# A decode step on one core: last values in three parts, output blocks as rows of 512, one product for the bias

## The chip, the core and the metric

The kernel runs on one core of a Trainium2 chip. The core has a matrix engine (TensorE, "PE" in the profile, with its weight loads listed apart as "PEld"), a vector engine (VectorE, DVE), a scalar engine (ScalarE, ACT), GpSimd (POOL) and a queue engine (SyncE, SP) that here issues nearly all transfers from device memory. Sixteen DMA engines move the data. On-chip data lies in SBUF; TensorE writes its products to PSUM, from where VectorE or ScalarE fetch them. The metric is the device time of one execution in microseconds; a time for a kernel is the median of its runs.

## What is computed

One token of 512 values passes two branches. The attention branch, cut to what matters:

```python
q = (xn @ wq)                       # 32 heads of 128
k = k_cache[:, :, Sk - 4096:, :]    # the last 4096 rows of every head
v = v_cache[:, :, Sk - 4096:, :]
p = softmax(q . k * Dh ** -0.5)
o = p @ v                           # 32 heads of 128, side by side: 4096 values
s = o @ wo                          # 4096 x 512
out = x + s * silu(B(xn))
```

`xn` is the normalised token and `B` a small two-layer branch with weights of 512x512, 512x1376 and 1376x512. Every head has its own keys and values, all bf16: 32 heads x 4096 rows x 128 values for K and again for V are 64 MiB, and `wq` and `wo` add 4 MiB each.

## The kernel before

**Loads.** All large loads go through `load` (line 77) on SP's queue in program order: the weights of `B`, `wq`, and then, for each step `s`, the K tile of head pair `s` and the V tile of head pair `h = s - 3` (`LAG`). A K or V tile holds two heads as 128 partitions x 64 columns x 128 values, 2 MiB. There are six K buffers and three V buffers. The output weights `wo` come between them: the block of heads 0 to 15 (`load_wo(0)`, 2 MiB) and of heads 16 to 23 (`load_wo(1)`, 1 MiB) in K buffers that have become free, heads 24 and 25 spread over 64 partitions (`load_few`), and the rows of heads 26 to 31 two heads at a time (`load_rows`, 256 KiB each). The last V tile comes in two parts, 48 and 16 columns (`CUT`), with the rows of heads 28 and 29 between the two and those of heads 30 and 31 behind.

**Scores.** Of every K tile, `nd(s)` columns are multiplied with q and summed on VectorE (`k_vector`, lines 309 and 311) and the others are transposed on TensorE into a buffer `pt` of the pool `ps_tr`, which has three, copied out by ScalarE (`k_turn`, lines 324 and 325) and multiplied by q on TensorE (`k_scores`, line 330).

**Softmax.** For a group of four heads, `sm_max` makes the maximum of each partition; `sm_turn` turns it on TensorE (line 355), takes the maximum of each head (line 357) and lays the scaled maxima out as a small matrix `md` (line 360). `sm_exp` spreads it over the partitions with two products into one PSUM tile `mb_ps`: ones times `md` (line 368), and a fixed parity pattern `par_t` times a fixed matrix `neg` of 0 and -1e30 (line 370), so that each partition sees only the heads whose values it holds. ScalarE copies the tile out (line 373) and takes the exponentials p with it as bias (line 377). `sm_den` and `sm_rden` make the reciprocal of the sum.

**Values.** `v_pair` multiplies p by a V tile: for most pairs 64 products with a V column block as weights and 2 columns of p (line 441), for four pairs p as weights and 512 columns of V (line 430). `v_out` scales the result by the reciprocal, one ScalarE instruction a head (line 461), into the columns of `o_blk`.

**Output product.** Heads 0 to 15 and 16 to 23 are first rearranged (`ox_spread`, `ox_pick`), heads 24 and 25 (the few block) also through `ox_few`. Then there are two forms of multiplying by `wo`. `y_wide` (line 498), used for heads 0 to 15 alone, makes one product of 512 columns for each of its 16 weight rows, into a PSUM row that ScalarE copies to `y_row` (line 504). `rows_add` (line 149), used for everything else, makes four products of 128 columns into partitions 0, 32, 64 and 96 of a PSUM tile `y_ps`, which stays open until the last head. `y_block` calls it for a block, `y_head` for one head, and a last call adds `y_row` to `y_ps`.

**Order.** The loop over `s` stands in a region in which the order on TensorE, VectorE and ScalarE is the order of the text. The last three steps, which hold V tiles 13, 14 and 15, are the ones the change touches most:

```python
sm_turn(LG); ox_spread(few_block); y_block(1); sm_exp(LG); ox_pick(few_block)
rows_add(y_ps, one_f, y_row, False); v_pair(h, v); v_out(2 * h, 2); ox_few(few_block)
sm_den(LG); sm_rden(LG)
...
y_block(few_block); v_pair(h, v); v_out(2 * h, 2)
...
for r in range(h_part, h_part + 2): y_head(r)
v_pair(h, v, 0, CUT)
for r in range(h_part + 2, H - 2): y_head(r)
v_pair(h, v, CUT, CP); v_out(2 * h, 2)
for r in range(H - 2, H): y_head(r)
```

After the region, VectorE multiplies `y_ps` by the gate and adds x (lines 607 and 609), and SP stores the result.

Of the kernel before, what the change touches and what calls it, by code (L numbers as in the profile page):

```python
# [8 lines left out]
P = 128  # L9
# [14 lines left out]
EARLY = 4  # L24
LATE = 14
MOVED = (1, 3)
CUT = 48


@with_exitstack  # L30
def kernel(
# [39 lines left out]
    ps_o = ctx.enter_context(tc.tile_pool(name="ps_o", bufs=1, space=PSUM))  # L71
    ps_y = ctx.enter_context(tc.tile_pool(name="ps_y", bufs=1, space=PSUM))
    sm_pool = ctx.enter_context(tc.tile_pool(name="sm", bufs=3))
    wts_guard = tc.tile_pool(name="wts", bufs=1)
    wts = wts_guard.__enter__()

# [19 lines left out]
    def load_kv(pool, cache, i, cuts=None):  # L96
        t = pool.tile([P, CP, Dh], BF16, tag="kv", name="kv")
        src = cache[0, 2 * i:2 * i + 2, W0:, :].rearrange("a (b c) d -> b a (c d)", b=P // 2)
        dst = t[:].rearrange("p c d -> p (c d)")
        cuts = cuts or (0, CP)  # L100
        for c0, c1 in zip(cuts, cuts[1:]):
            load(dst[:, c0 * Dh:c1 * Dh], src[:, :, c0 * Dh:c1 * Dh])
            if c0 == 0 and c1 < CP:
                load_rows(H - 4, 2)
        return t

# [154 lines left out]
    for c in range(2):  # L261
# [10 lines left out]

    par = const.tile([P, 2], FP32, name="par")
    nc.vector.tensor_reduce(out=par[:], in_=ident_f[:].rearrange("p (b a) -> p a b", a=2), axis=AX.X,
                            op=ALU.max)
    par_t = const.tile([2, P // 2, 2], FP32, name="par_t")
    nc.vector.tensor_copy(out=par_t[:], in_=ident_f[0:2, 0:2].unsqueeze(1).to_broadcast([2, P // 2, 2]))
    neg = const.tile([2, 2, 2], FP32, name="neg")  # L280
    nc.vector.tensor_scalar(out=neg[:], in0=ident_f[0:2, 0:2].unsqueeze(1).to_broadcast([2, 2, 2]),
                            scalar1=-1.0, scalar2=1e30, op0=ALU.add, op1=ALU.mult)


# [66 lines left out]
    def sm_turn(g):  # L351

        s = st[g]
        mt_ps = ps_misc.tile([2, P], FP32, tag="misc", name="mt_ps")
        nc.tensor.transpose(mt_ps[:], s["m1"][:], ident_f[:])  # L355
        mx = sm_pool.tile([2, 2], FP32, tag="mx", name="mx")
        nc.vector.tensor_reduce(out=mx[:], in_=mt_ps[:].rearrange("r (b a) -> r a b", a=2), axis=AX.X,
                                op=ALU.max)
        s["md"] = sm_pool.tile([2, 2, 2], FP32, tag="md", name="md")
        nc.vector.scalar_tensor_tensor(out=s["md"][:],  # L360
                                       in0=ident_f[0:2, 0:2].unsqueeze(2).to_broadcast([2, 2, 2]),
                                       scalar=-scale, in1=mx[:].unsqueeze(1).to_broadcast([2, 2, 2]),
                                       op0=ALU.mult, op1=ALU.mult)

    def sm_exp(g):
        s = st[g]
        mb_ps = ps_misc.tile([P, G], FP32, tag="misc", name="mb_ps")
        nc.tensor.matmul(mb_ps[:], lhsT=ones_f[0:2, :], rhs=s["md"][:].rearrange("k r a -> k (r a)"),  # L368
                         start=True, stop=False)
        nc.tensor.matmul(mb_ps[:], lhsT=par_t[:].rearrange("k b a -> k (b a)"),  # L370
                         rhs=neg[:].rearrange("k r a -> k (r a)"), start=False, stop=True)
        mb = sm_pool.tile([P, G], FP32, tag="mb", name="mb")
        nc.scalar.copy(out=mb[:], in_=mb_ps[:])  # L373
        s["pT"] = sm_pool.tile([P, 2, CP, 2], BF16, tag="pT", name="pT")
        s["sum"] = sm_pool.tile([P, G], FP32, tag="sum", name="sum")
        for i in range(G):
            nc.scalar.activation(out=s["pT"][:, i // 2, :, i % 2], in_=s["S"][:, i // 2, :], func=ACT.Exp,  # L377
                                 scale=scale, bias=mb[:, i:i + 1], accum_out=s["sum"][:, i:i + 1])
# [73 lines left out]
    def v_out(h, n):  # L452
        g, hl = divmod(h, G)
        b = [i for i, (h0, _) in enumerate(blocks) if h >= h0][-1]
        if b not in o_blk:
            o_blk[b] = sm_pool.tile([P, blocks[b][1]], BF16, tag=f"o{b}", bufs=1, name="o")
            if b == few_block:
                nc.gpsimd.memset(o_blk[b][:], 0.0)
        c = h - blocks[b][0]
        for k in range(n):  # L460
            nc.scalar.mul(o_blk[b][:, c + k:c + k + 1], st[g]["oT"][:, hl + k:hl + k + 1],  # L461
                          st[g]["rden"][:, hl + k:hl + k + 1])
# [31 lines left out]


    y_row = small.tile([1, D], FP32, name="y_row")

    def y_wide(i):
        n = blocks[i][1]
        yr_ps = ps_misc.tile([1, D], FP32, tag="misc", name="yr_ps")  # L500
        for t in range(n):
            nc.tensor.matmul(yr_ps[:], lhsT=ox_blk[i][:, t:t + 1], rhs=wo_blk[i][:, t, :], start=(t == 0),
                             stop=(t == n - 1))
        nc.scalar.copy(out=y_row[:], in_=yr_ps[:])

    def y_block(i):
        for t in range(8):
            rows_add(y_ps, ox_blk[i][:, t:t + 1], wo_blk[i][:, t, :], False)

    def y_head(h):  # L510
        rows_add(y_ps, o_blk[few_block][:, h - few_h:h - few_h + 1], wo_row(h), h == H - 1)

    NP = H // 2
    LG = H // G - 1
    region = tc.manual_schedule(engines={mybir.EngineType.PE, mybir.EngineType.DVE,
# [3 lines left out]
    for s in range(NP + LAG):  # L519
        h = s - LAG  # L520
        last = h == NP - 1
        kn = load_kv(k_pool, A_k_cache, s) if s < NP else None
        if s == LAG:
            wts_guard.__exit__(None, None, None)
            v_pool = ctx.enter_context(tc.tile_pool(name="v", bufs=V_BUFS))
            wo_blk[few_block] = v_pool.tile([64, 8, D], BF16, tag="wo_few", bufs=1, name="wo_few")
            nc.gpsimd.memset(wo_blk[few_block][:], 0.0)
            wo_rows = v_pool.tile([P, H - h_part, D], BF16, tag="wo_rows", bufs=1, name="wo_rows")
        if last:
            load_rows(h_part, 2)  # L530
            v = load_kv(v_pool, A_v_cache, h, (0, CUT, CP))
        elif h >= 0:
            v = load_kv(v_pool, A_v_cache, h)
        if h in (7, 12):
            load_wo(h // 12)
        if h == 11:
            load_few()
        if last:
            load_rows(H - 2, 2)

        if s < NP:
            turn = [s // 2 - 1] if s % 2 == 0 and s > 0 else []
            k_open(s)
            k_vector(s, kn, 0)
            k_turn(s, kn)
            for g in turn:
                sm_turn(g)
            if s % 2 == 1 and s >= 3:
                sm_den((s - 3) // 2)
                sm_rden((s - 3) // 2)  # L550
            k_scores(s)
            if s % 2 == 1:
                sm_own(s // 2)
            for g in turn:
                sm_exp(g)
            if s in (12, 15):
                ox_spread(s // 14)
            if s == 11:
                v_add(3)
                v_out(12, 4)  # L560
            k_vector(s, kn, 1)
            if h >= 0:
                v_pair(h, v)
            if s in (12, 15):
                ox_pick(s // 14)
            if s == 13:
                y_wide(0)
            if s % 2 == 1:
                sm_max(s // 2)
            g = (h - 1) // 2  # L570
            if h > 0 and h % 2 == 1 and g not in MOVED:
                v_out(G * g, G)
            if h % 2 == 0 and h > 0 and g in MOVED and g != 3:
                v_add(g)
                v_out(G * g, G)
            if s == NP - 1:
                v_out(2 * h, 2)
        elif s == NP:

            sm_turn(LG)  # L580
            ox_spread(few_block)
            y_block(1)
            sm_exp(LG)
            ox_pick(few_block)
            rows_add(y_ps, one_f, y_row, False)
            v_pair(h, v)
            v_out(2 * h, 2)
            ox_few(few_block)
            sm_den(LG)
            sm_rden(LG)  # L590
        elif not last:
            y_block(few_block)
            v_pair(h, v)
            v_out(2 * h, 2)
        else:
            for r in range(h_part, h_part + 2):
                y_head(r)
            v_pair(h, v, 0, CUT)
            for r in range(h_part + 2, H - 2):
                y_head(r)  # L600
            v_pair(h, v, CUT, CP)
            v_out(2 * h, 2)
            for r in range(H - 2, H):
                y_head(r)
# [36 lines left out]
```

## Time and profile before

| | us |
|---|---|
| median of 4 runs | 195.93 (195.86 to 196.92) |
| the profiled execution | 196.05 |
| its span, first to last instruction | 194.3 |
| PE busy, of the span | 141.0 (73%) |
| DVE busy | 138.5 (71%) |
| ACT busy | 83.9 (43%) |
| moved by DMA | 79.16 MB, mean 407 GB/s |
| mean granted TensorE clock | 0.707 of full speed |

The profile is of one execution. Its page gives busy times over the whole span, slices of the span, the chain of work that ended last, and groups of instructions by source line with count, busy time, mean duration and the idle time before them. Further views of the same trace list instructions in order of time, the chain in order of time, and the busy time, granted clock and DMA share of any stretch. A matmul's listed duration includes its own latency, so that matmuls overlap in the list and the distance between starts is what one costs in a series. Times in what follows are microseconds from the start of the span.

### The profile page before, as it was taken

The page shows a single profiled execution, that of the slowest core. Times are in us where ns is not written, and L with a number is a line of the kernel's source. Part 1 is how long each engine was busy: PE and PEld are TensorE (multiplying, and loading weights), DVE is VectorE, ACT ScalarE, POOL GpSimd, SP SyncE. Part 2 cuts the span into 40 slices and gives each one's busy share as a digit, 9 for nine tenths or more (in the row PEclk, how much of TensorE's full clock was granted, in tenths as well). Part 3 has the DMA queues.
Part 4 walks back from the last instruction along what each step waited for, and adds up shares of the span by engine and source line. Part 5 has one row for each costly group of instructions (what it writes and reads, how often), then busy time and mean ns, then how long its engine had stood idle before and what let it go on. Part 6 is the DMA issues. An engine that isn't in the chain of part 4 may idle for free.

```text
span 194.3 us, 4894 instructions
## 1 busy us (share of the span) xinstructions
PE 141.0 (73%) x2188; PEld 112.0 (58%) x2188; DVE 138.5 (71%) x160; ACT 83.9 (43%) x183; POOL 6.2 (3%) x13
## 2 busy tenths in 40 slices
PE   0549779877787993497886979286767997959651
PEld 0444469867787943257885254086757556947540
DVE  1550119969489999999999998098999977881001
ACT  2003019887946905235746053161546057823000
POOL 2110007000000000000000000000000000000000
PEclk9999966797558699588555596855556697575555
DMA  5999899999999999999999999999999999999960
GB/s 212 403 498 432 381 425 425 427 425 432 425 432 425 427 425 432 432 425 432 425 432 428 432 432 422 428 432 428 425 428 422 432 425 432 422 435 423 413 265 2
DMA packets 6909, 79.16 MB, mean 407 GB/s; under 512 B 872, under 2 KB 1736, under 8 KB 2120
## 3 DMA queue, kind: packets, MB, share of 16 engines
q1 hardware_dynamic: 6736, 78.84, 95.6%
q8 instruction: 17, 0.28, 0.5%
q14 instruction: 4, 0.03, 0.0%
q10 hardware_dynamic: 152, 0.00, 0.0%
HBM read 78.84 MB, written 0.00 MB: 406 GB/s over the span
## 4 chain that ended last, share of the span: by engine, by line
DMA 42%; DVE 24%; PE 15%; ACT 11%; issue 4%; SPq 2%; POOL 1%; DVEq 0%; ACTq 0%; POOLq 0%
DMA kv<-in_A_k_cache_dram 32%; DVE S L311 14%; ACT kt L325 10%; DMA kv<-in_A_v_cache_dram 8%; DVE prod L309 7%; PE pt L324 3%; PE oT L441 2%; DMA x_bf<-in_A_x_dram 2%; PE qT_ps L239 2%; SPq L78 2%; PE hr_ps L223 2%; PE a_ps L212 1%; PE qb_ps L251 1%; PE oT L448 1%; PE hr_ps L220 1%
## 5 line engine op out<-in xcount | busy, mean ns | idle before, releaser
L311 DVE TENSOR_REDUCE S<-prod 128x20 f32<-128x2560 bf16 (+2 forms) x32 | 79.6, 2486 | 1.1
L325 ACT COPY kt<-pt 128x1024 bf16<-128x1024 bf16 x58 | 54.6, 1024 | 27.2 <-PE pt L324 27.2
L324 PE MATMUL pt<-ident_bf,kv 128*128 128x128 bf16 x464 | 44.5, 278 | 10.0 <-DMA kv<-in_A_k_cache_dram 8.0
L309 DVE TENSOR_TENSOR prod<-kv,q_bc 128x2560 bf16<-128x2560 bf16 (+2 forms) x32 | 42.2, 1318 | 10.3 <-DMA kv<-in_A_k_cache_dram 8.0
L324 PEld LDWEIGHTS <-kv 128*128 128x128 bf16 x464 | 40.5, 129 | 13.5 <-DMA kv<-in_A_k_cache_dram 9.0
L330 PE MATMUL sT<-qT_bf,kt 128*128 128x2 bf16 x464 | 18.0, 165 | 10.8 <-ACT kt L325 10.5
L441 PE MATMUL oT<-pT,kv 128*128 128x2 bf16 x768 | 22.1, 165 | 4.3 <-DMA kv<-in_A_v_cache_dram 4.2
L441 PEld LDWEIGHTS <-kv 128*128 128x128 bf16 x768 | 21.3, 102 | 5.8 <-DMA kv<-in_A_v_cache_dram 5.8
L330 PEld LDWEIGHTS <-kt 128*128 128x128 bf16 x464 | 16.8, 102 | 13.2 <-ACT kt L325 12.7
L430 PE MATMUL ov<-kv,pT 128*8 128x512 bf16 x64 | 19.6, 474 | 0.0
L461 ACT ACTIVATE o<-oT,rden 128x1 bf16<-128x1 f32 x32 | 6.0, 263 | 17.5 <-PE oT L441 11.2
L430 PEld LDWEIGHTS <-pT 128*8 128x8 bf16 x64 | 6.2, 102 | 12.0 <-issue 8.1
L377 ACT ACTIVATE pT<-S,mb 128x64 bf16<-128x64 f32 x32 | 10.9, 357 | 0.2
L373 ACT COPY mb<-mb_ps 128x4 f32<-128x4 f32 x8 | 1.3, 162 | 18.4 <-PE mb_ps L370 18.4
L368 PE MATMUL mb_ps<-md,ones_f 2*128 2x4 f32 x16 | 4.0, 316 | 5.7 <-DVE md L360 5.7
L607 DVE TENSOR_TENSOR y<-y_ps,g_row 128x128 f32<-128x128 f32 x1 | 0.3, 292 | 9.7 <-PE y_ps L152 9.7
L368 PEld LDWEIGHTS mb_ps<-md,ones_f 2*128 2x128 f32 x16 | 3.4, 261 | 6.2 <-issue 6.1
L226 DVE COPY hr<-hr_ps 1x512 f32<-1x512 f32 x1 | 0.7, 679 | 7.9 <-PE hr_ps L223 7.9
L377 ACT ACTIVATION_READ_ACCUMULATOR pT<-S,mb 128x1 f32 x32 | 6.0, 187 | 0.0
L157 PE MATMUL ln_ps<-x_f,ones_f 128*128 128x4 f32 x4 | 1.2, 364 | 5.9 <-DVE x_f L180 4.8
L215 ACT ACTIVATE a_bf<-a_ps 128x10 bf16<-128x10 f32 x1 | 0.2, 179 | 12.1 <-PE a_ps L212 12.1
L355 PE MATMUL mt_ps<-ident_f,m 128*2 128x128 f32 x8 | 2.7, 340 | 3.5 <-DVE m L349 3.5
(116 smaller groups left out, 106.5 us busy)
## 6 DMA issues: line engine op xcount, KB each, us to landing
kv<-in_A_k_cache_dram SPq DMA_DIRECT2D x16, 2048.0 KB, 28.9
kv<-in_A_v_cache_dram SPq DMA_DIRECT2D x15, 2048.0 KB, 25.9
wq_sb<-in_A_wq_dram SPq DMA_DIRECT2D x1, 4096.0 KB, 17.8
wo<-in_A_wo_dram SPq DMA_DIRECT2D x1, 2048.0 KB, 29.0
kv<-in_A_v_cache_dram SPq DMA_DIRECT2D x1, 1536.0 KB
w_sb<-in_B_w_dram SPq DMA_DIRECT2D x1, 1376.0 KB, 6.8
w_sb<-in_B_w_dram SPq DMA_DIRECT2D x1, 1024.0 KB
wo<-in_A_wo_dram SPq DMA_DIRECT2D x1, 1024.0 KB
```

The lines of the kernel that those rows point to most:

```text
L78: return tc.keep_in_program_order(nc.sync.dma_start(out=dst, in_=src))
L223: nc.tensor.matmul(hr_ps[:], lhsT=a_bf[0:m, i:i + 1], rhs=w4_sb[0:m, i, :], start=False, stop=(i == len(chunks) - 1))
L309: nc.vector.tensor_tensor(out=prod[:, 0:m, :], in0=kn[:, rows, :], in1=q_bc[:, s:s + 1, :].to_broadcast([P, m, Dh]), op=ALU.mult)
L311: nc.vector.tensor_reduce(out=st[s // 2]["S"][:, s % 2, rows], in_=prod[:, 0:m, :], axis=AX.X, op=ALU.add)
L324: nc.tensor.transpose(pt[:, i, :], kn[:, n + b + i, :], ident_bf[:])
L325: nc.scalar.copy(out=kts[s][:, b:b + w, :], in_=pt[:, 0:w, :])
L330: nc.tensor.matmul(st[s // 2]["sT"][:, s % 2, c, :], lhsT=kt[:, c, :], rhs=qT_bf[:, 2 * s:2 * s + 2], start=True, stop=True)
L368: nc.tensor.matmul(mb_ps[:], lhsT=ones_f[0:2, :], rhs=s["md"][:].rearrange("k r a -> k (r a)"), start=True, stop=False)
L377: nc.scalar.activation(out=s["pT"][:, i // 2, :, i % 2], in_=s["S"][:, i // 2, :], func=ACT.Exp, scale=scale, bias=mb[:, i:i + 1], accum_o ...
L430: nc.tensor.matmul(s["ov"][32 * r:32 * r + 8], lhsT=s["pT"][:, r, c:c + 4, :].rearrange("p i a -> p (i a)"), rhs=v[:, c:c + 4, :], start=F ...
L441: nc.tensor.matmul(s["oT"][:, 2 * r:2 * r + 2], lhsT=v[:, c, :], rhs=s["pT"][:, r, c, :], start=(c == 0), stop=(c == CP - 1))
L461: nc.scalar.mul(o_blk[b][:, c + k:c + k + 1], st[g]["oT"][:, hl + k:hl + k + 1], st[g]["rden"][:, hl + k:hl + k + 1])
```

## The change

There are four edits.

1. The last V tile is loaded and multiplied in three parts (32, 24 and 8 columns). The rows of heads 28 and 29 are loaded after the second part, and the four heads 26 to 29 are multiplied between the second and the third.
2. Blocks 1 (heads 16 to 23) and 2 (the few block) are multiplied by `y_wide` as rows of 512, into one PSUM row that both share and that lies in the pool of the transposes. `y_keep` copies the first block's row to `y_row` on ScalarE as before, and adds the row of the other two to it on VectorE; only then is `y_row` added to `y_ps`. Block 1 now stands behind the bias product, not ahead of it; the four products that add `y_row` move from ahead of V tile 13's products to behind V tile 14's.
3. The bias of p is one product: `md` is a fixed tile of four rows, two written for each group and two holding the -1e30 pattern, and `par_t` has four rows to match. Constants for it are made on VectorE at the start (one reduction more).
4. For heads 26 and up, `v_out` is one VectorE instruction for two heads in place of two on ScalarE.

A tile `pad` of 64 bytes a partition is added to one pool; with the other changes of tiles the working tiles behind it move by 96 bytes, and the K and V buffers stay where they were.

```diff
+    small.tile([P, 32], BF16, name="pad")
...
             load(dst[:, c0 * Dh:c1 * Dh], src[:, :, c0 * Dh:c1 * Dh])
-            if c0 == 0 and c1 < CP:
+            if len(cuts) > 2 and c1 == cuts[-2]:
                 load_rows(H - 4, 2)
...
-    par_t = const.tile([2, P // 2, 2], FP32, name="par_t")
-    nc.vector.tensor_copy(out=par_t[:], in_=ident_f[0:2, 0:2].unsqueeze(1).to_broadcast([2, P // 2, 2]))
-    neg = const.tile([2, 2, 2], FP32, name="neg")
+    two = const.tile([4, 1], FP32, name="two")
+    nc.vector.tensor_reduce(out=two[:], in_=ident_f[0:4, 0:2], axis=AX.X, op=ALU.max)
+    par_t = const.tile([4, P // 2, 2], FP32, name="par_t")
+    nc.vector.tensor_scalar(out=par_t[:], in0=ident_f[0:4, 2:4].unsqueeze(1).to_broadcast([4, P // 2, 2]),
+                            scalar1=two[:], scalar2=None, op0=ALU.add)
+    md = const.tile([4, 2, 2], FP32, name="md")
...
-        nc.tensor.matmul(mb_ps[:], lhsT=ones_f[0:2, :], rhs=s["md"][:].rearrange("k r a -> k (r a)"),
-                         start=True, stop=False)
         nc.tensor.matmul(mb_ps[:], lhsT=par_t[:].rearrange("k b a -> k (b a)"),
-                         rhs=neg[:].rearrange("k r a -> k (r a)"), start=False, stop=True)
+                         rhs=md[:].rearrange("k r a -> k (r a)"), start=True, stop=True)
...
+        if h >= h_part:
+            nc.vector.tensor_tensor(out=o_blk[b][:, c:c + n], in0=st[g]["oT"][:, hl:hl + n],
+                                    in1=st[g]["rden"][:, hl:hl + n], op=ALU.mult)
+            return
...
     def y_wide(i):
         n = blocks[i][1]
+        if i != few_block:
+            yr["ps"] = ps_tr.tile([1, D], FP32, tag="pt", name="yr_ps")
         for t in range(n):
-            nc.tensor.matmul(yr_ps[:], lhsT=ox_blk[i][:, t:t + 1], rhs=wo_blk[i][:, t, :], start=(t == 0),
-                             stop=(t == n - 1))
-        nc.scalar.copy(out=y_row[:], in_=yr_ps[:])
-
-    def y_block(i):
-        for t in range(8):
-            rows_add(y_ps, ox_blk[i][:, t:t + 1], wo_blk[i][:, t, :], False)
+            nc.tensor.matmul(yr["ps"][:], lhsT=ox_blk[i][:, t:t + 1], rhs=wo_blk[i][:, t, :],
+                             start=(i != few_block and t == 0), stop=(i != 1 and t == n - 1))
+
+    def y_keep(i):
+        if i == 0:
+            nc.scalar.copy(out=y_row[:], in_=yr["ps"][:])
+        else:
+            nc.vector.tensor_tensor(out=y_row[:], in0=y_row[:], in1=yr["ps"][:], op=ALU.add)
+            rows_add(y_ps, one_f, y_row, False)
...
+    cuts = (0, 32, 56, CP)
...
-            v = load_kv(v_pool, A_v_cache, h, (0, CUT, CP))
+            v = load_kv(v_pool, A_v_cache, h, cuts)
...
             sm_turn(LG)
             ox_spread(few_block)
-            y_block(1)
             sm_exp(LG)
+            y_wide(1)
             ox_pick(few_block)
-            rows_add(y_ps, one_f, y_row, False)
             v_pair(h, v)
             v_out(2 * h, 2)
...
-            y_block(few_block)
+            y_wide(few_block)
             v_pair(h, v)
             v_out(2 * h, 2)
+            y_keep(few_block)
         else:
-            for r in range(h_part, h_part + 2):
-                y_head(r)
-            v_pair(h, v, 0, CUT)
-            for r in range(h_part + 2, H - 2):
-                y_head(r)
-            v_pair(h, v, CUT, CP)
+            for c0, c1 in zip(cuts, cuts[1:]):
+                if c1 == CP:
+                    for r in range(h_part, H - 2):
+                        y_head(r)
+                v_pair(h, v, c0, c1)
             v_out(2 * h, 2)
```

## The prediction

> **What bounds the kernel now.** I read the page's slices first, for the DMA row.
>
> ```profile
> DMA  5999899999999999999999999999999999999960
> ```
>
> All slices but the first two and the last two are at 90% or more: the 16 DMA engines are never out of work while the caches stream. The page's list of DMA issues says how far ahead they are fed: a K tile lands 28.9 us after its issue, a V tile after 25.9. A delay of a few microseconds on TensorE, VectorE or ScalarE in the middle of the kernel therefore costs nothing. Only what follows the last bytes, and what the engines cannot finish before them, sets the end. So I went to the end of the chain of waits (start, us, what).
>
> ```profile
> 173.62 15.42 DMA kv<-in_A_v_cache_dram
> 189.04 0.05 issue
> 189.09 0.60 PE oT L441 x16
> 189.69 0.02 issue
> 189.72 0.27 ACT o L461
> 189.99 0.04 issue
> 190.03 0.46 PE y_ps L152 x7
> 190.49 0.02 issue
> 190.51 0.30 DVE y L607
> ```
>
> The last part of V lands at 189.04; 16 products, one scaling, eight output products and two VectorE operations follow. Then the timeline, for how much room TensorE has before that (start, us, idle before it in brackets).
>
> ```profile
> 152.32 5.25 PE L502 MATMUL yr_ps<-wo,ox 128*1 128x512 bf16 x16
> ...
> 174.52 1.02 PE L152 MATMUL y_ps<-wo,ox 128*1 128x128 bf16 x32
> ...
> 180.50 1.02 PE L152 MATMUL y_ps<-wo_few,of 64*1 64x128 bf16 x32
> ...
> 182.96 1.86 PE L441 MATMUL oT<-pT,kv 128*128 128x2 bf16 x64 [1.44 <-DMA kv<-in_A_v_cache_dram]
> ...
> 187.23 1.44 PE L441 MATMUL oT<-pT,kv 128*128 128x2 bf16 x48 [2.10 <-DMA kv<-in_A_v_cache_dram]
> ```
>
> TensorE waits for V at 182.96 and 187.23. The two output blocks that the change rewrites cost 1.02 us each, in front of those waits. Last, the windows, cut every 3.41 us because the granted clock changes only at such steps (after the times: length, PE and PEld busy, DVE, ACT, POOL, then the clock).
>
> ```profile
> 145.42:148.83 3.41, 3.04 (x31) 3.04 (x32) 3.34 (x4) 1.97 (x3) 0.00 (x0) 0.50 0.99 418
> 148.83:152.25 3.42, 2.40 (x89) 2.23 (x86) 3.39 (x4) 1.18 (x2) 0.00 (x0) 1.00 1.00 426
> 152.25:155.66 3.41, 3.41 (x14) 1.03 (x11) 3.21 (x4) 0.00 (x0) 0.00 (x0) 0.50 1.02 437
> 155.66:159.07 3.41, 3.35 (x33) 1.99 (x32) 3.35 (x2) 1.46 (x3) 0.00 (x0) 1.00 0.97 406
> ...
> 176.14:179.55 3.41, 2.98 (x76) 2.35 (x76) 0.49 (x2) 1.59 (x9) 0.00 (x0) 0.50 1.03 432
> 179.55:182.97 3.42, 1.63 (x36) 1.27 (x36) 0.34 (x2) 0.41 (x2) 0.00 (x0) 0.50 0.99 409
> ```
>
> Half clock throughout the tail. The first block's 16 wide products straddle a change: eight start in the window at 0.50 (0.42 us each), the other eight after 155.66 at 1.00 (finished by 157.5, so 0.22 us each).
>
> **What the change costs: the data's side.** The bytes stay the same. From 182.96 to 187.23, 1.75 MiB landed (two output rows, 48 columns of V), 0.43 MB/us; from there to 189.09, 0.75 MiB in smaller pieces, 0.42. With cuts at 32 and 56 the same rate gives the first part at 186.0, the second at 187.85, rows 28 and 29 at 188.45, the third part at 189.1, rows 30 and 31 at 189.7. [...] The two rates just shown differ by 0.04 us over the second stretch[...]. I take +0.05. The added issue on SP (0.54 to 0.59 us each) comes 15 us before its data and delays rows 30 and 31's issue only.
>
> After the third part: 8 products instead of 16 save 0.23 (0.60 less the 0.165 of one product's own latency, over 15 starts, is 0.029 each). The scaling moves from ScalarE's 0.27 to one VectorE operation on 128x2; the small VectorE rows (L197, 128x4 out of PSUM; L360) take 0.15, so 0.12 less. The heads 30 and 31 could begin at 189.7, and their rows land at 189.7, formerly covered by the slower scaling: start 189.75 instead of 190.03. Their eight products no longer wait for a second scaling: 0.41 for 0.46. **Floor: -0.3 us**, if TensorE is ready at 189.1.
>
> **TensorE's side.** The maximum's VectorE steps end at 175.09 as now (same order on VectorE). Then:
> - One bias product instead of two: a pair of passes takes 0.54 (L370's weight loads, 162.47 to 162.99): done at 175.65. The other bias products are hidden under the cache stream.
> - Block 1: 8 wide products instead of 32 narrow ones. Now the narrow ones fill the wait for the maximum; after, the block stands behind the bias product. At half clock 8 x 0.427 (3.41/8) = 3.4: done at 179.05. V tile 13 has been there since 177.65, so its products, until now released by DMA, are late by 1.4.
> - Tile 13's 64 products, 1.78 (their weight loads): 180.9. Sorting and denominator, as now from 179.43 to 180.50, 1.07: 182.0.
> - Block 2: 8 wide products: 3.4 at half clock (185.4) or 1.73 at full (183.7). Tile 14, landed at 182.96: 1.78, to 187.2 or 185.5.
> - A new wait: the row is added by VectorE behind the scaling of heads 28 and 29, and TensorE's four row products wait for it, with the whole of tile 15 queued behind them. 1x512 from PSUM took 0.68 (L226); with the scaling, the last product's latency and hand-overs 1.07, plus 0.25 for the row products (starts 176.88 to 177.1): 188.5 or 186.8.
> - 32 columns 0.9; 24 columns 0.67; four heads, 16 products at 0.027 (32 in 1.02, less latency), 0.43. At full clock the second part is awaited (187.85) and TensorE is ready at 188.95, before the data at 189.1. At half clock it is ready at 190.5: late by 1.4, so the end moves by -0.3 + 1.4, less the 0.1 that the rows' landing had cost: **+1.0**.
>
> So the clock in block 2 decides. [...] By the trace alone (half clock over the whole tail) the answer is +1.0[...]. [...] by transposes (L324), which stream like the wide products: 2.69 us of them (from 63.50) and 2.72 (from 56.67) raised the clock, 2.62 (from 101.05 and from 135.18) did not; once up, 1.64 us of L430's wide products (from 66.91) kept it, 1.39 us of transposes (from 32.78) did not. [...] On this trace's grid block 1 fills 2.9 us of 176.14 to 179.55: the clock rises at 179.55. Block 2 has then only 1.0 us before 182.97, too little to hold it: four and a half products at full clock, the rest at half, done at 184.45. From there TensorE is ready for the third part at 189.55, 0.45 late; the heads start at 190.15, end 190.56 against 190.49: **+0.1**. On other grids that raise the clock the sum lies mostly from -0.3 to +0.3; I take **+0.15**.
>
> Costed at nothing: the constants (one small VectorE reduction more, 0.28 by L276), ahead of a stage in which DMA is full; the block sum's buffer among the transposes' three, since its 0.57 us copy at 157.61 precedes the third transpose tile; the scalings moved off ScalarE in the tail, idle there. The pad leaves K and V where they were and shifts working tiles by 96 bytes; no row shows what that does, I take 0, and a change of 1% on the long VectorE rows would still be hidden. TensorE's program is 104 rows shorter; the page's 17 instruction packets (0.5% of 16 engines: 0.9 us each) may meet a different DMA engine late: -0.3 to +0.3, taken as 0.
>
> **Forecast.** The profiled execution took 196.05 (span 194.3 and 1.75 around it): 196.2 after. The median of the runs, 195.93, is 0.12 lower: **196.1**.
>
> **Rivals.**
> - The floor: block 2 runs wholly at full clock, or the stalls are shorter than I count, and the end stays with the last bytes: -0.3, 195.6. For it: only 0.45 us separates it on this grid. Against it: block 2 must start early in a raised window.
> - **Slower:** block 1 is split by a window's edge, no window holds 2.65 us of it, and both blocks run at half clock: +1.0, 196.9. Block 1 lasts 3.4, so about 1.5 of the 3.41 possible positions of the grid raise the clock after it; a few more raise it within block 2. It decides from the point where block 2 ends later than about 183.9. Against: this trace's grid, if it returns.
> - The edits hide altogether, or the DMA engines' end moves by itself: 195.6 to 196.3.
>
> **How the numbers follow.** Forecast 0.42, floor 0.17, half clock 0.33, the last 0.08. Their times run from 195.5 to 196.9, and with stalls mis-sized by 0.2 to 197.2; I take 195.4 to 197.2. About 0.5%, 0.98 us, is what a measurement can tell from no change: 194.95 to 196.91. The half-clock case lies on the upper edge, so somewhat over half of it counts as slower, with a little of the forecast's: 0.27. Faster needs three times the floor: 0.05.
>
> **What would show it.** Granted clock in the window where the second block's wide products run, and their spacing (0.22 or 0.43); tile 13 and 14's products no longer released by DMA; idle time before the row products ended by VectorE, about 1 us; the third part released by DMA (floor) or following the heads at once (late); the last heads released by a DMA of output rows. I am wrong if tile 14 still waits for its data, if the third part lands later than 189.3, or if the wide products run faster than their windows' clock allows.

## The result and the profile after

| | before | after |
|---|---|---|
| median, us | 195.84 (63 runs) | 196.75 (44 runs) |
| lowest and highest | 195.70, 197.43 | 195.78, 198.87 |
| the profiled execution | 196.05 | 195.99 |
| its span | 194.3 | 194.1 |

The ratio is 1.0041, 95% interval 1.0026 to 1.0055: slower by about 0.4%, 0.9 us. But the median is not the time of any run. The 44 runs fall into two groups of 22, 195.78 to 196.34 and 197.16 to 198.87, with nothing between, and the median is the middle of that gap. (Some executions of either kernel take about 1.2 us longer, 9 of the 63 before, at 196.92 to 197.43; they are part of the upper group's spread.)

The profiled execution is of the lower group. Its chain of waits, from the single bias product on (start, us, what):

```profile
175.09 0.55 PE mb_ps L371 x2
175.64 3.50 PE yr_ps L509 x8
179.14 0.17 PE ox_ps L482
179.31 1.62 PE oT L442 x64
...
181.39 0.36 PE den_ps L384 x2
181.74 2.23 PE yr_ps L509 x8
183.97 1.82 PE oT L442 x64
...
185.97 0.59 DVE y_row L516
186.56 0.04 issue
186.60 0.60 PE y_ps L152 x8
187.20 1.59 PE oT L442 x56
188.79 0.52 PE y_ps L152 x8
189.31 0.32 PE oT L442 x8
```

Before, this chain was one DMA wait of 15 us; now it is TensorE's own series. Nothing in it waits for V any more: tile 13's products follow block 1, tile 14's follow block 2, and the first two parts of tile 15 (56 products in one row) follow the row products. TensorE reaches the third part at 189.31, about when its data are there (189.1). Block 1's eight products took 3.50 us, block 2's eight only 2.23. The wide products alone, in the windows of the clock (after the times: length, PE and PEld busy, the clock, DMA share and GB/s):

```profile
172.78:176.19 3.41, 0.62 (x2) 0.21 (x3) 0.50 1.02 437
176.19:179.60 3.41, 2.95 (x7) 0.64 (x5) 0.50 0.98 411
179.60:183.02 3.42, 1.35 (x7) 0.54 (x8) 1.00 1.01 408
```

The second window held 2.95 us of block 1; the clock rose from 0.50 to 1.00 at its end, and block 2 began at full clock.

### The profile page after: what moved, and what is told of

Same layout as the page of the kernel before. It is cut to its first block, busy times and chain, and to the rows that moved or that the text cites. A ratio compares the mean times of both kernels' runs of the same rounds, so it can differ in the third digit from the quotient of the medians.

```text
span 194.1 us, 4764 instructions
## 1 busy us (share of the span) xinstructions
PE 141.0 (73%) x2124; PEld 108.3 (56%) x2124; DVE 139.7 (72%) x165; ACT 82.7 (43%) x177; POOL 6.3 (3%) x13
## 4 chain that ended last, share of the span: by engine, by line
DMA 34%; DVE 27%; PE 22%; ACT 9%; issue 4%; SPq 1%; POOL 1%; DVEq 0%; ACTq 0%; POOLq 0%
DMA kv<-in_A_k_cache_dram 32%; DVE S L315 15%; DVE prod L313 8%; ACT kt L329 8%; PE pt L328 4%; PE oT L442 4%; PE yr_ps L509 3%; DMA x_bf<-in_A_x_dram 2%; PE qT_ps L239 2%; PE hr_ps L223 2%; PE a_ps L212 1%; PE qb_ps L251 1%; SPq L78 1%; PE oT L449 1%; PE hr_ps L220 1%
## 5 line engine op out<-in xcount | busy, mean ns | idle before, releaser
L315 DVE TENSOR_REDUCE S<-prod 128x20 f32<-128x2560 bf16 (+2 forms) x32 | 79.6, 2487 | 1.1
L509 PE MATMUL yr_ps<-wo,ox 128*1 128x512 bf16 x24 | 8.9, 546 | 0.0
L371 PE MATMUL mb_ps<-md,par_t 4*128 4x4 f32 x16 | 3.7, 298 | 6.8 <-DVE md L363 6.1
L466 ACT ACTIVATE o<-oT,rden 128x1 bf16<-128x1 f32 x26 | 4.7, 264 | 6.7 <-PE oT L449 4.8
L371 PEld LDWEIGHTS mb_ps<-md,par_t 4*128 4x128 f32 x16 | 3.1, 244 | 7.4 <-issue 5.1
L462 DVE TENSOR_TENSOR o<-oT,rden 128x2 bf16<-128x2 f32 x3 | 0.5, 159 | 8.0 <-PE oT L442 8.0
```

Of the source, the lines that this page charges most:

```text
L315: nc.vector.tensor_reduce(out=st[s // 2]["S"][:, s % 2, rows], in_=prod[:, 0:m, :], axis=AX.X, op=ALU.add)
L509: nc.tensor.matmul(yr["ps"][:], lhsT=ox_blk[i][:, t:t + 1], rhs=wo_blk[i][:, t, :], start=(i != few_block and t == 0), stop=(i != 1 and t ...
```

## The experiments

Theory: TensorE's series sets the end, and whether the clock's grid lets block 1 raise the clock for block 2 makes the two groups. Rivals: the groups come from another edit; the wait for VectorE's sum or block 1's 3.5 us costs by itself; the groups come from outside TensorE. "Before" below is the kernel before in the same set of runs; its medians lie between 195.89 and 196.02, so levels from different sets compare to about 0.1 us.

**The changed kernel again.** No edit.

> The changed kernel as it is, one more look. Clock theory: if the windows' edges leave less than about 2.65 us of block 1 in each window, the clock is 0.50 over block 2, its eight products take 3.4 to 3.5 us, and the run is at 197.2 to 197.6; if a window holds more than 2.7 us, the clock rises and the run is at 195.8 to 196.3.

It took 197.56, an execution of the upper group. Its windows, for the wide products alone:

```profile
173.26:176.68 3.42, 1.03 (x3) 0.34 (x4) 0.50 1.02 436
176.68:180.09 3.41, 2.54 (x6) 0.51 (x4) 0.50 1.01 418
180.09:183.50 3.41, 1.45 (x4) 0.45 (x5) 0.50 0.97 396
```

Measured from the start of block 1, the edges lie 0.4 us later than in the first profile: 2.54 us in the fullest window, and the clock stayed at 0.50 over block 2. The chain of the same execution:

```profile
175.72 3.50 PE yr_ps L509 x8
...
182.12 3.50 PE yr_ps L509 x8
185.62 1.81 PE oT L442 x64
...
187.61 0.59 DVE y_row L516
188.20 0.04 issue
188.25 0.60 PE y_ps L152 x8
188.85 1.59 PE oT L442 x56
190.44 0.52 PE y_ps L152 x8
190.96 0.32 PE oT L442 x8
```

Line by line it is the first chain with block 2 at 3.50 instead of 2.23 (and the denominator's products at 0.56 instead of 0.36, tile 13's at 1.70 instead of 1.62); everything behind is 1.65 us later. The DMA engines moved 419 GB/s from 15 to 25 us and 430 from 170 to 180 (419 and 429 in the first profile), and at the end TensorE waits for no data: the 0.22 us before the third part's weight loads (190.89) end with no releaser that the profile shows, and the last heads (191.51) are released by VectorE. It is TensorE's series that is late.

A third execution of it:

> The changed kernel as it is, a third look: a window with more than about 2.65 us of block 1's products goes with a time of 195.8 to 196.3, none with 197.2 to 197.6.

It took 197.16, although a window held all eight products of block 1 and the clock rose:

```profile
176.23:179.64 3.41, 3.27 (x8) 0.85 (x8) 0.50 1.02 435
179.64:183.06 3.42, 0.95 (x5) 0.32 (x5) 1.00 0.96 386
```

So the expectation, as written, was missed. The reason is at the end of its chain:

```profile
176.02 15.08 DMA wo_rows<-in_A_wo_dram
191.10 0.04 issue
191.14 0.41 PE y_ps L152 x6
```

The last output rows landed at 191.10, not at 189.7 (in this execution the transfers had lost time early; see the last section). An execution can be in the upper group's range without the clock being the cause.

**Both blocks narrow again**, all else as changed:

```diff
+            y_block(1)
             sm_exp(LG)
-            y_wide(1)
             ox_pick(few_block)
+            rows_add(y_ps, one_f, y_row, False)
...
-            y_wide(few_block)
+            y_block(few_block)
             v_pair(h, v)
             v_out(2 * h, 2)
-            y_keep(few_block)
```

> Both blocks of the output product go back to four narrow products a weight row, and the row of block 0 is added where it was before; the three parts, the single bias product and the VectorE scaling stay. If the two groups of times of the changed kernel come from the granted clock over the wide rows: one group of times, at 195.5 to 195.7 (0.2 to 0.3 under the kernel before), since TensorE is then ready for every part of the last tile. If the slow group comes from the parts, the bias or the scaling: still two groups, 1.5 us apart.

One group: 19 of 22 runs at 195.48 to 195.85, median of all 195.69 where before had 195.96, ratio 0.9985 (0.9974 to 0.9997). The loss and the two groups come with the second edit, the wide blocks and their sum. In its timeline (idle before in brackets) TensorE waits for data ahead of tile 14, of each part of the last tile, and of the last heads:

```profile
182.73 1.87 PE L442 MATMUL oT<-pT,kv 128*128 128x2 bf16 x64 [1.33 <-DMA kv<-in_A_v_cache_dram]
...
185.81 1.01 PE L442 MATMUL oT<-pT,kv 128*128 128x2 bf16 x32 [1.21 <-DMA kv<-in_A_v_cache_dram]
...
187.63 0.80 PE L442 MATMUL oT<-pT,kv 128*128 128x2 bf16 x24 [0.80 <-DMA kv<-in_A_v_cache_dram]
...
188.93 0.29 PEld L442 LDWEIGHTS <-kv 128*128 128x128 bf16 x8 [0.28 <-DMA kv<-in_A_v_cache_dram]
...
189.59 0.38 PE L152 MATMUL y_ps<-wo_rows,o 128*1 128x128 bf16 x8 [0.28 <-DMA wo_rows<-in_A_wo_dram]
```

The last line is the landing of rows 30 and 31, which has taken the place of the scaling as what the last heads wait for.

**The wide blocks alone**, on the kernel before (edit 2 without the others):

```diff
-            y_block(1)
             sm_exp(LG)
+            y_wide(1)
             ox_pick(few_block)
-            rows_add(y_ps, one_f, y_row, False)
...
-            y_block(few_block)
+            y_wide(few_block)
             v_pair(h, v)
             v_out(2 * h, 2)
+            y_keep(few_block)
```

> The kernel before with the second edit alone: wide rows for blocks 1 and 2 and the sum on VectorE; two parts, two bias products and ScalarE's scaling as before. Clock theory: two groups again, the lower at 195.9 to 196.4, the upper 1.5 us above it. If the slow group needs the other edits: one group at 195.9 to 196.2.

Eight runs: one at 196.02, six at 197.03 to 197.41, one at 198.71; ratio 1.0054 (1.0023 to 1.0084). The upper level appears without the other edits. Its profile, at 197.27, had 2.12 us of block 1 in the fullest window and half clock, 3.50 us for each block. There the row products did not wait for the sum (in its chain they follow tile 14's products at 187.85, with no step of VectorE between), so the upper level doesn't need that wait. Eight runs don't measure how the runs divide.

**Only one block wide.** First block 1 wide and block 2 narrow, `y_block(few_block)` in place of `y_wide(few_block)`:

> Block 1 stays a row of 512, block 2 goes back to narrow products; the wait for the VectorE sum stays. Clock theory: block 1 always runs at half clock (its 3.4 us are in every time already), and block 2 then costs 1.02 us[...], so tile 14 is met about when it lands and there is one group at 195.5 to 195.8. If block 1's 3.4 us or the wait for the sum is what costs: 196.3 or more in all runs.

Ten of 14 runs at 195.67 to 195.98, the others scattered to 197.89; median 195.94, ratio 1.0000 (0.9975 to 1.0024). Against before, block 1's 3.4 us and the wait for the sum, alone, cost nothing that is measured; against the kernel with both blocks narrow, in the same set, the ten runs are 0.2 later (medians 195.90 and 195.68). (In its profile, at 197.39, the transfers were late as in the third execution above; I read nothing from its chain.) Then block 2 wide and block 1 narrow, `y_block(1)` ahead of `sm_exp(LG)`:

> Block 1 goes back to narrow products ahead of the bias product, block 2 stays wide, with the sum behind tile 14. Block 2 then always runs at half clock, 3.5 us, but it starts about 1.6 us earlier. Clock theory with the sum of TensorE's series: tile 15 begins at about 187.1 as in the profile of the fast group, one group at 195.8 to 196.1. If wide rows at half clock cost time wherever they stand: 197 or more.

Eleven of 13 runs at 195.96 to 196.21, median 196.01. Block 2 ran at half clock (0.50 in both of its windows), but began at 180.48. From its chain:

```profile
180.48 3.50 PE yr_ps L509 x8
...
187.21 1.59 PE oT L442 x56
```

Tile 15 began at 187.21, the same as in the lower group of the changed kernel. Block 2 alone at half clock costs little: 0.08 over before, and 0.3 over narrow blocks with the last tile in two parts (195.74, same set, further below). It takes both in the series to cost 1.5.

**Block 1 split**, so that no window is filled:

```diff
-            y_wide(1)
+            y_wide(1, 0, 4)
             ox_pick(few_block)
             v_pair(h, v)
+            y_wide(1, 4, 8)
```

> Block 1's eight wide products are split: four ahead of tile 13's products and four behind them. Work and waits are the same, but no 3.41 us window before block 2 holds more than about 2.1 us of wide products. Clock theory: block 2 always starts at half clock, so the fast group at 195.8 to 196.3 vanishes and nearly all runs lie at 197.2 to 197.6. If the two groups come from something that differs from run to run outside TensorE (the DMA engines, say), both stay, about half and half.

All four runs, 198.00 to 198.10; no lower group. The wide products in the windows:

```profile
176.35:179.76 3.41, 1.51 (x5) 0.26 (x4) 0.50 1.00 418
179.76:183.17 3.41, 2.06 (x6) 0.41 (x5) 0.50 0.97 391
```

The clock stayed at 0.50, as expected; the level is 0.6 above the upper group's median, since here, against the expectation, the waits did change: the block's rearranged columns share a buffer with the next block's, whose last VectorE step had to wait for the second half (3.37 us idle before it, until 181.24; block 2 began at 182.62 instead of 182.12). Four runs of one kind would happen by chance one time in sixteen if the halves were still even; together with the clock in the profile I take it as shown that here the spacing of block 1's products decides whether the clock rises.

**The wait for the sum.** Two ways to take it off the path. The sum and its row products behind the second part of the last tile:

```diff
             v_pair(h, v)
             v_out(2 * h, 2)
-            y_keep(few_block)
...
                 if c1 == CP:
+                    y_keep(few_block)
                     for r in range(h_part, H - 2):
```

> Only the VectorE sum and its four row products move, from ahead of the last tile to behind its second part. The wait of about 1.1 us leaves TensorE's series. If that wait is on the path in the slow group, the slow group comes down by about 1 us, from 197.5 to 196.5, and the fast group stays at 195.8 to 196.1. If the wait was hidden, both groups stay where they are.

Two groups of ten, 196.16 to 196.40 and 196.82 to 196.97, and two runs above. The upper came down by 0.6, not 1; the lower went up by 0.25, not expected. Its profile is of the upper group (196.88): at most 2.33 us of block 1 in a window, and 3.50 us for each block, at half clock. The wait that could be saved was 0.77 us (187.43 to 188.20 in the upper group's chain above), and in the chain here the first part still waits 0.25 us for VectorE's scaling of the tile that shares its PSUM buffer, and row products and heads take 1.06 us together ahead of the last part: the work was moved, only the wait was saved. The other way leaves the row products and puts VectorE's sum ahead of its scaling (`rows_add` is taken out of `y_keep`):

```diff
             y_wide(few_block)
+            y_keep(few_block)
             v_pair(h, v)
             v_out(2 * h, 2)
-            y_keep(few_block)
+            rows_add(y_ps, one_f, y_row, False)
```

> VectorE's sum stands ahead of its scaling of heads 28 and 29, so it runs while TensorE multiplies tile 14; the four row products stay where they are but no longer wait. In the profile of the slow group they waited 0.77 us (187.43 to 188.20). If TensorE's series sets the end: the slow group comes down by 0.7 to 0.8, from 197.5 to 196.7, and the fast group, by then bound by the last bytes, to 195.6 to 195.9. If the wait was not on the path: no move.

Groups at 195.70 to 195.95 (six runs) and 196.58 to 197.03 (eight); the upper group down by 0.8, as expected. Its profile is of the lower group (195.83): a window held all of block 1, 3.41 us, and block 2 began at full clock, 1.00. The wait was on the path. Two groups remain, so it is not what splits them.

**The third part.** Narrow blocks with the last tile in two parts, heads 26 and 27 ahead of the first and 28 and 29 ahead of the second:

```diff
-    cuts = (0, 32, 56, CP)
+    cuts = (0, 48, CP)
```

> Narrow blocks, single bias product and VectorE scaling as in the first experiment, but the last tile in two parts again (48 and 16 columns). By the prediction's terms the third part is worth 0.23 us less the 0.07 by which the rows' landing then decides: 195.8 to 195.9 where the first experiment had 195.69. If the three parts bring nothing: 195.7.

195.74 (195.52 to 197.01, 21 runs) against before at 195.93. Since this is within noise of the three parts, both were run once more side by side:

> Narrow blocks with all other edits once more, beside the next run on the same chip: 195.6 to 195.7, 0.2 to 0.3 under the kernel before.

> The same with the last tile in two parts, once more. By the prediction's terms 0.16 above the run beside it (0.23 for eight products less, 0.07 given back to the landing of the last rows); if the third part brings nothing, equal to it within 0.05.

195.80 and 195.78. Over both sets, runs under 196.2: median 195.70 with three parts (30 runs), 195.73 with two (27). Whatever the third part is worth, it is not the 0.16 of my sum; I can't tell 0.03 from nothing.

The narrow kernels, with three parts or with two, are the fastest of all that ran, but against before they are at the edge of what can be told: with three parts 0.9985 in one set and 0.9997 (0.9977 to 1.0017) in the other, with two 0.9995 (0.9980 to 1.0010) and 0.9998 (0.9978 to 1.0018).

## Why the prediction was right, and where it was not

**Bound and lever.** Right. The end is set by the last bytes or by TensorE's series after 175 us, and the clock over block 2 decides how late that series is. For the grid of the trace before, the sum gave 189.55 as the moment when TensorE is ready for the third part; the first profile, on nearly the same grid, had 189.31, and block 1 ended at 179.14 (179.05 in the sum), block 2 at 183.97 (184.45, as it began 0.3 earlier), the row products began at 186.60. That the two moments lie so close is in part luck: block 2 ended 0.48 earlier than in the sum and the wait behind tile 14 was 0.25 shorter, while the row products and the heads took 0.44 longer. That execution, 195.99, and the lower group's median of 196.0 are the forecast's case (196.1), not the floor's (195.6).

**The clock.** In the trace before, the granted clock changes 21 times, from 25.95 us to 172.73, and any two changes lie a whole multiple of 3.413 us apart. Its transposes, which gave the bounds, start one after the other as the wide products do: 0.107 us for 128 columns at half clock and 0.056 at full, where 512 columns take 0.427 and 0.216. Products of 2 columns did not hold the clock up: the windows from 148.83 and from 169.31 ran at 1.00, with 83 and 95 of them and no transposes of K, and were followed by 0.50. The bounds were worth more than that trace's half clock taken as lasting, by which no execution would be in the lower group. They held for block 1 in all profiles in which it is wide: 2.95 us and more of it in a window raised the clock (four profiles), 2.54 and less did not (four). The grid did not lie alike from execution to execution: a window's edge fell at 175.60, 176.19, 176.68 and 177.54 in four of these profiles.

**What failed: the chances and the size of the half-clock case.** I gave it 0.33, though the working itself said that only 1.5 of 3.41 us of grid positions let block 1 raise the clock, that is, that 56% do not. I counted on block 2 to make up for it; but by the same bounds a window must first hold some 2.65 of block 2's 3.5 us at half clock, and then little of it is left to gain. Half of the runs are in the upper group (22 of 44, a few of them for the other reason). And it costs 1.5 us, not 1.0 (197.56 in the profile of the upper group, 196.05 in that of the kernel before). In the slow chain the last heads ended at 191.93, not 191.5. The terms that were too small: the row products by 0.35 (0.60 for 0.25), the two blocks by 0.1 each, the four heads by 0.09, and the chain began 0.07 later; the wait for the sum, put at 1.07, was 0.25 shorter, which hid part of this.

The largest, the row products, I had put at the distance of their first and last start. The trace before lists them so:

```profile
176.88 0.60 PE L152 MATMUL y_ps<-y_row,ones_f 1*1 1x128 f32 x8
...
177.65 1.86 PE L441 MATMUL oT<-pT,kv 128*128 128x2 bf16 x64 [0.18 <-DMA kv<-in_A_v_cache_dram]
```

What followed them waited for a V tile, so their cost to it could not be seen, and of the listed 0.60 I counted the starts alone. In the upper group's profile no data are awaited behind them:

```profile
188.25 0.60 PE L152 MATMUL y_ps<-y_row,ones_f 1*1 1x128 f32 x8 [0.83 <-DVE y_row L516]
...
188.78 1.66 PE L442 MATMUL oT<-pT,kv 128*128 128x2 bf16 x56
```

The next products begin 0.53 after the first (0.60 in the chain, which counts to the end of the last). That the distance between starts is what a matmul costs holds inside a series (wide products at half clock are listed at 0.63 us and start 0.43 apart), not at its end.

So the median, predicted as one case's time, fell in the gap of a mixture: 196.75 where 196.1 was named. That it lies within my 195.4 to 197.2 says little for the working, since 21 of the 44 runs lie above 197.2.

**DMA side.** Right as to arrival: in the first profile the five pieces landed at 185.9, 187.8, 188.4, 189.1 and 189.7, predicted were 186.0, 187.85, 188.45, 189.1 and 189.7, and the trace before had 189.04 and 189.7 for the last V part and the last rows. So the added transfer cost at most 0.05 us between these two executions, as was estimated from the two rates of the trace before; in the timeline of narrow blocks the same pieces came about 0.2 earlier than predicted. The landing of rows 30 and 31 became what the last heads wait for, as forecast. In the DMA row of the page before, the slices under 90% are the first, the fifth (80 to 90%, 381 GB/s) and the last two, not the first two and the last two. The floor of -0.3 came, with both blocks narrow, as -0.27 and -0.09 in two sets; with two parts it is -0.19 and -0.11, so it doesn't rest on the third part.

**The third part's 0.16** is not seen. With two parts the end follows a chain of 0.60, 0.17 and 0.41 us from the landing at about 189.0; with three it waits for the landing of the last rows. The heads end 0.3 apart in the two profiles, but 0.14 of this is that V landed at 189.03 in one and at 188.89 in the other, and the profiled runs lie 0.14 above and 0.07 below their medians. The medians differ by 0.03, and no run explains where the rest of the 0.16 goes.

**Costed at nothing.** Right as far as the runs show: the kernels with narrow blocks have the constants, the buffer and the shifted tiles, and are not slower than before; VectorE's long sums took 2820 ns a piece (128x20 of L315), as before.

## What to carry to other kernels

A median is not a prediction's target when one step depends on a clock that changes on a grid, and the grid does not lie alike from execution to execution (here an edge at 175.60 in one, at 177.54 in another): work out the time on each side of the bound that the windows show (here between 2.54 and 2.95 us of wide products) and how many positions of the grid lie on each, and look at all runs before trusting one profile. Replacing short products that overlap (32 in 1.02 us) by long ones (8 in 2.23 us at best and 3.50 at half clock) was free here only where TensorE had that slack at half clock. And where a group of products is followed by a DMA wait, the distance of its starts is only a lower bound of what it will cost in a series; its listed duration is the safer term (0.19, 0.53 and 0.60 us for the row products).

## What the runs showed of the hardware

- A short group of products held up what follows for longer than its starts tell. In the first profile of the changed kernel the eight row products start within 0.19 us (186.60 to 186.79), and the V products behind them 0.53 after the first. It is not the V products alone that come so late: with the sum moved behind the second part, the heads' products follow, which go to the same four partitions as the row products (with 128 rows of weights, not one), and they begin 0.54 after the first:

```profile
189.18 0.60 PE L152 MATMUL y_ps<-y_row,ones_f 1*1 1x128 f32 x8
...
189.72 0.59 PE L152 MATMUL y_ps<-wo_rows,o 128*1 128x128 bf16 x16
```

Why the next group begins so late stays open.

- The profile's busy time did not tell the clock. In the trace before TensorE was busy for the whole of one window at half clock, but only 1.04 us of it with transposes, the rest with products of 2 and 4 columns; the clock did not rise after it:

```profile
90.81:94.22 3.41, 3.41 (x50) 3.41 (x47) 3.38 (x4) 0.72 (x4) 0.00 (x0) 0.50 0.98 418
94.22:97.63 3.41, 2.74 (x41) 2.51 (x39) 3.38 (x2) 2.84 (x3) 0.00 (x0) 0.50 1.01 428
```

- Block 2's products, which use 64 rows, raised no clock in the one window that held as much of them, 2.95 us, as the window of 128-row products that had raised it in the first profile (block 1 split):

```profile
183.17:186.59 3.42, 2.95 (x7) 0.61 (x5) 0.50 0.93 376
```

The V products behind it, 64 from 186.12 in 1.81 us and 56 from 189.35 in 1.59, took what they took at 0.50 in the first profile (1.82 and 1.59; in the trace before, 64 are listed at 1.86 us at 0.50 and at 1.75 at 1.00). It is one window, not tried further.

- Time that the transfers lost early was not made up. In the third execution of the changed kernel the DMA engines moved 374 GB/s from 15 to 25 us of the span where the first had 419, both moved 427 to 430 from 40 us to 180, and the last output rows landed 1.4 us later (191.10 against 189.7). The profile with block 1 alone wide, whose last rows landed at 191.31, shows 328 GB/s from 15 to 20 us. The kernel before, whose last rows landed at 189.7, moved 419 there. The cause stays open.
